# Low parts of stage-two weights and of the token matrix, summed on TensorE; six weight slots; transfers held back

## The chip, the cores and the metric

The kernel runs on one core of one Trainium2 chip. The time is that of one execution on the device, in microseconds. A core has a matrix engine (TensorE, PE in the profile), three engines for elementwise work (VectorE or DVE, ScalarE or ACT, GpSimd or POOL), and SyncE (SP), whose queue issues every transfer of this kernel.

## The reference

Three stages run over 8 batches of 576 tokens: an attention with softmax on each side, a feed-forward layer with a gate over tokens, and one with a convolution over tokens.

```python
# stage one: 8 heads of 64
q_s = softmax(q, over d);  k_s = softmax(k, over tokens)
x = q_s @ (k_s^T @ v)                        # per batch and head, then 576 x 512
# stage two
h = gelu(x @ w_in)                           # 512 -> 1024
u, v = h[..., :512], h[..., 512:]
v_n = (v - mean) / sqrt(var + 1e-6) * g_ln
v_s = w_sg @ v_n + b_sg                      # 576 x 576 over the tokens
x = x + (u * v_s) @ w_out
# stage three
h = relu(x @ w_in2)                          # 512 -> 1024
out = (h * sigmoid(conv3(h))) @ w_out2       # three taps over the tokens
```

## The kernel before

Each product of two float32 matrices is made of three matmuls in the one-piece type F32R. A matrix is held as a high part (its value rounded to F32R) and a low part (what the rounding left), and `mm3` adds high x high, high x low and low x high. So every operand has to be split before it is used. For activations this is a copy on ScalarE for the high part and a subtraction for the low one. The weights `w_in`, `w_out`, `w_in2`, `w_out2` arrive as 64-bit numbers: `split` (a "job") loads 512 columns of 64-bit words, takes them apart with integer operations on VectorE and ScalarE into a leading value `a` and a remainder `lf`, rounds `a` to `hi` on ScalarE, and makes the low part in two elementwise steps, `a - hi` and then `+ lf`, each on VectorE or GpSimd as the string `MODES_` says.

Stage two has 12 such jobs: 0 to 3 are the `v` half of `w_in`, 4 to 7 its `u` half, 8 to 11 `w_out`. A job needs a slot of SBUF for its raw words and its `a`; there are three, in buffers that later hold the tokens of batch 1 (`xh`, `xl`) and one operand of batch 1 (`lt`), so job 3 waits for job 0's slot. The token matrix `w_sg` is loaded in four blocks of 128 rows and one of 64 into `x2s`, and split by `sg_split` and `sg_tail` into `sgh`, `sgl` and `rhs`; `b_sg` goes into two rows of `rhs`.

Work of stages one and two in a batch is a list of 29 groups: `hv` (tokens times the `v` half, 12 matmuls of 512 columns each, four tiles and a pair tile for the left-over 64 tokens), `hu` (the `u` half, eight units of 12 matmuls of 288 columns), `mx` (the token matrix, 14 matmuls), `wo` (times `w_out`, 12 matmuls). `insert` puts stage one of later batches between them: `attend_k` and `attend_q` (the softmax steps on VectorE, GpSimd and ScalarE), `back_kv` (k times v on TensorE), `xt` and `xt_left` (q times that, which makes the tokens of the next batch). Stage three follows for all batches.

Nothing runs in the order of the code. `Plan` records every instruction, gives each a cost, and works out for each how late it may start (`late`) from where its consumer stands among TensorE's units. `Plan.order` then plays the program forward: a free engine takes the waiting instruction with the earliest `late`; TensorE takes the first unit of the next eight that would hardly stall. Each engine then has that fixed order on the chip. SP is such an engine too, with one line to memory of 200 KB per us. All instructions are issued from one line (L394 in the rows below), so they are told apart by the names of their tiles.

Two names in the rows need a word: `xLh` is also the tile of the identity matrix at the start, and `sgh` and `sgl` first hold q and k of batch 0.

Of the kernel before, what the change touches and what calls it, by code (L numbers as in the profile page):

```python
# [30 lines left out]
class View:  # L31
# [46 lines left out]
    def region(self):  # L78
        n = self.tile.n
        ids = self.ids  # L80
        col = ids.reshape(ids.shape[0], -1)[0] % n if ids.size < 4000 else np.unique(ids[0]) % n
# [60 lines left out]
class Plan:  # L142
    WINDOW = 8

    def __init__(self, real):
# [55 lines left out]
    def price(self, n, out, ins):  # L201
# [9 lines left out]
        elif e == "pe":  # L211
            m = size(out)
            if name == "transpose":
                n.cost = 0.22
            elif ins[0].tile.dtype == F32:
                n.cost = 0.09 if m == 65 else 0.71 if m == 512 else 0.19
            else:
                n.cost = max(0.111, 0.0045 + m * 0.000447)
            n.lat = n.cost + 0.17
        elif e == "act":  # L220
            n.cost = 0.13 + cols * 0.00086
            n.lat = n.cost + 0.12
            f = args_func(n)
            n.table = {"Gelu_apprx_tanh": "g", "Exp": "e", "Sigmoid": "s"}.get(f)
        elif e == "pool":
            if "tensor" in name:
                n.cost = 0.55 if cols == 1 else 0.2 + cols * (0.0008 if name == "tensor_copy" else 0.00195)
# [27 lines left out]
    def order(self):  # L255
# [41 lines left out]
        def start(n, t):  # L297
# [3 lines left out]
            if n.eng == "dve" and n.shared and poolend[0] > t:  # L301
                more = min(cost, poolend[0] - t) * 0.8
                cost, lat = cost + more, lat + more
# [5 lines left out]
            if n.eng == "dve" and n.shared:  # L309
                vecend[0] = t + cost  # L310
            if n.eng == "sp":
                s = max(t + 0.4, wire[0])
                wire[0] = s + n.kb / 200
                lat = wire[0] + 1.9 - t
            n.t, n.done = t, t + lat
            free[n.eng] = t + cost
# [24 lines left out]
        while events:  # L341
# [4 lines left out]
            while again:  # L346
                again = False
                for k in self.real:
                    if free[k] > t + 1e-9:
                        continue  # L350
                    if k == "pe":
# [22 lines left out]
                        continue  # L374
                    can = [n for n in queue[k] if n.ready <= t + 1e-9]
                    if can:
                        key = lambda n: (n.late + (2.0 if n.table and n.table != table[0] else 0.0), n.i)
# [25 lines left out]
def attn_gated_conv_kernel(ctx, tc, q, k, v, q0, k0, w_in, g_ln, w_sgT, b_sg, w_out, w_in2, conv_w, w_out2, out):  # L403
# [47 lines left out]
    def split(slot, src, hi, lo, n, modes, stores=(), behind=None):  # L451
# [24 lines left out]
        if hi is None:  # L476
            dve.tensor_tensor(lo, a, lf, ALU.add)
            return
        modes[0].tensor_tensor(a, a, r32(hi), ALU.subtract)
        modes[1].tensor_tensor(lo, a, lf, ALU.add)  # L480
# [38 lines left out]
    lt2 = [p1.tile([128, DM], F32R, name=f"lt2{i}") for i in range(2)]  # L519
    vn_hi = p1.tile([128, 4, DM], F32R, name="vnh")  # L520
    vn_lo = p1.tile([128, 4, DM], F32R, name="vnl")
    kvd = p1.tile([128, 4, 128], F32, name="kvd")
# [309 lines left out]
    xL = {}  # L832
    ident = p1.tile([128, 256 * 2], F32, tag="xLh")[:, 0:128]
    make_identity(nc, ident.real())
# [91 lines left out]

    bview = b_sg.rearrange("(o t) -> o t", o=1)
# [10 lines left out]
    def sg_bias():  # L938
        for e in range(2):
            o = 64 - 64 * e  # L940
            sp.dma_start(sgs[o:o + 2, 1], bview.to_broadcast([2, S]))

# [27 lines left out]
    xt_copy(0)  # L970
    for i, jb in enumerate(jobs):
        split(slots[i % 3], *jb, MODES[i])
        if i == 7:
            split(csl[0], conv_v, None, cw, 3 * NFC, None)
    s_sg()

    def sg_split(c):
        act.activation(sg["hi"][:, c], sgs[:, c % 2], AF.Copy)
        E[CFG['sgl'][c]].tensor_tensor(sg["lo"][:, c], sgs[:, c % 2], r32(sg["hi"][:, c]), ALU.subtract)
        if c < 3:  # L980
            sg_load(c + 2)
        if c == 3:
            sg_bias()

    def sg_tail():
        act.activation(rhs1, sgs[:, 0], AF.Copy)
        bsh = sgs[:, 0].bitcast(F32R)
        for e in range(2):
            r = slice(64 * e, 64 * e + 64)
            E[CFG['rh'][e]].tensor_tensor(rhs2[e][r], sgs[r, 0], r32(rhs1[r]), ALU.subtract)  # L990
        for e in range(2):
            o = 64 - 64 * e
            act.activation(bsh[o:o + 2], sgs[o:o + 2, 1], AF.Copy)
            dve.tensor_tensor(rhs2[e][o:o + 2], sgs[o:o + 2, 1], r32(bsh[o:o + 2]), ALU.subtract)
            dve.tensor_copy(rhs2[e][o:o + 1], r32(bsh[o:o + 1]))

    w2 = {}

    NW = 256
    wsl = p1.tile([128, 1792], F32, name="wsl")  # L1000
    parts = [((wsl[:, 512 * i:512 * i + 512], wsl[:, 1024 + NW * i:1024 + NW * i + NW]), wsl[:, 1536:1792]) for i in range(2)]
# [106 lines left out]
    for b in range(B):  # L1108
# [196 lines left out]
```

## Time and profile before

| what | value |
|---|---|
| median of 3 runs | 1012.88 us (1011.97 to 1016.14) |
| profiled execution, its own time | 1012.38 us |
| its span in the profile | 1010.6 us |
| mean granted clock of TensorE | 0.966 |
| TensorE busy | 932.2 us, 92% of the span |
| VectorE busy | 758.2 us, 75% |
| ScalarE, GpSimd busy | 471.7 us, 386.6 us |

The span is what the trace covers; the execution's own time is 1.8 us longer. Busy shares are means over stages: stages one and two of all batches run to about 600 us, stage three from there. A clock of 1.00 is 2.4 GHz, and 0.50 is 1.2 GHz. A wait in the rows is the time that an engine stood before an instruction, with the instruction that ended it.

### The profile page before, as it was taken

What the parts mean: (1) busy time and instruction counts of PE and PEld (TensorE: products, weight loads), DVE (VectorE), ACT (ScalarE), POOL (GpSimd) and SP (SyncE); (2) the same over time, 40 slices, a digit from 0 to 9 for tenths busy, and PEclk for the clock granted to TensorE, in tenths of its full rate; (3) what the DMA queues carried; (4) which work ended last, traced back from release to release, by engine and by line L of the source; (5) the groups of instructions that cost most, each with busy time, mean ns of one, the idle gap of its engine ahead of it and who ended that gap; (6) DMA issues with size and microseconds to landing.
All of it is one profiled execution on the core that took longest, in us unless ns stands there. A gap on an engine that the chain in (4) does not pass through costs nothing. (4 is left out here: it accounts for less than half of the span.)

```text
span 1010.6 us, 16155 instructions
## 1 busy us (share of the span) xinstructions
PE 932.2 (92%) x6080; PEld 836.1 (83%) x6080; DVE 758.2 (75%) x1361; ACT 471.7 (47%) x913; POOL 386.6 (38%) x469
## 2 busy tenths in 40 slices
PE   5456689999998998999999999999999999999998
PEld 3246578898887987989889999898999899989996
DVE  7999989878898895895763539977677757775663
ACT  5546434766755637545451315434343434343432
POOL 5666465645465552643540104442222312210000
PEclk9676989999999998999999999999999999999999
DMA  9702514251462442614327452332211211010001
GB/s 285 226 28 84 167 72 144 94 153 52 127 192 81 165 116 73 215 53 159 103 96 240 149 163 114 119 111 74 73 68 68 89 58 69 22 42 11 22 22 52
DMA packets 52326, 107.41 MB, mean 106 GB/s; under 512 B 5140, under 2 KB 28692, under 8 KB 48664
## 3 DMA queue, kind: packets, MB, share of 16 engines
q1 hardware_dynamic: 52248, 106.38, 32.6%
q8 instruction: 47, 0.77, 0.3%
q14 instruction: 31, 0.25, 0.1%
HBM read 70.85 MB, written 35.52 MB: 105 GB/s over the span
## 5 line engine op out<-in xcount | busy, mean ns | idle before, releaser
L394 PE MATMUL mm<-xh,w2h 128*128 128x288 f32 x512 | 151.3, 295 | 0.0
L394 PE MATMUL mm<-xh,w2l 128*128 128x288 f32 x512 | 151.1, 295 | 0.0
L394 PE MATMUL mm<-xl,w2h 128*128 128x288 f32 x512 | 150.6, 294 | 0.0
L394 DVE SCALAR_TENSOR_TENSOR cv<-h,cw,cv 128x576 f32<-128x576 f32 x128 | 117.5, 918 | 4.0
L394 ACT ACTIVATE cv<-cv 128x576 f32<-128x576 f32 x64 | 43.9, 686 | 138.2 <-DVE cv L394 138.2
L394 PE MATMUL acc<-wAh,yl 128*128 128x512 f32 x256 | 101.5, 396 | 0.0
L394 PE MATMUL acc<-wAh,yh 128*128 128x512 f32 x256 | 101.4, 396 | 0.0
L394 PE MATMUL acc<-wAl,yh 128*128 128x512 f32 x256 | 101.0, 394 | 0.0
L394 PEld LDWEIGHTS mm<-xl,w2h 128*128 128x128 f32 x512 | 96.6, 189 | 2.5
L394 PEld LDWEIGHTS mm<-xh,w2h 128*128 128x128 f32 x512 | 96.1, 188 | 2.5
L394 PEld LDWEIGHTS mm<-xh,w2l 128*128 128x128 f32 x512 | 96.3, 188 | 0.0
L394 PE MATMUL mm<-xh,wAh 128*128 128x288 f32 x256 | 80.7, 315 | 15.6 <-ACT wAh L394 11.3
L394 PE MATMUL mm<-sgh,vnh 128*128 128x288 f32 x256 | 81.8, 319 | 8.6 <-DVE xl L394 8.6
L394 DVE TENSOR_TENSOR yl<-cv,yh 128x576 fp32r<-128x576 f32 x64 | 51.9, 810 | 47.9 <-ACT yh L394 44.7
L394 PE MATMUL mm<-xh,wAl 128*128 128x288 f32 x256 | 77.6, 303 | 4.9 <-POOL wAl L394 4.8
L394 PE MATMUL acc<-gh,wouth 128*128 128x288 f32 x256 | 80.9, 316 | 0.3 <-ACT gh L394 0.3
L394 DVE TENSOR_TENSOR cv<-cv,h 128x576 f32<-128x576 f32 x64 | 51.8, 809 | 38.0 <-ACT cv L394 37.9
L394 PE MATMUL acc<-gh,woutl 128*128 128x288 f32 x256 | 76.6, 299 | 3.6 <-DVE woutl L394 3.6
L394 PE MATMUL acc<-gl,wouth 128*128 128x288 f32 x256 | 77.3, 302 | 2.8 <-DVE gl L394 2.7
L394 PE MATMUL mm<-xl,wAh 128*128 128x288 f32 x256 | 77.4, 302 | 0.0
L394 PE MATMUL mm<-sgh,vnl 128*128 128x288 f32 x256 | 77.1, 301 | 0.3 <-DVE vnl L394 0.3
L394 POOL TENSOR_TENSOR q<-q,qm 128x512 f32<-128x512 f32 x56 | 63.0, 1151 | 37.1 <-DVE qm L394 30.9
(188 smaller groups left out, 2533.0 us busy)
## 6 DMA issues: line engine op xcount, KB each, us to landing
vt<-in_v SPq DMA_DIRECT2D x8, 1152.0 KB, 11.5
x2d<-x2s SPq DMA_DIRECT2D x16, 576.0 KB, 4.0
out<-ot SPq DMA_DIRECT2D x32, 256.0 KB, 2.1
kt<-in_k SPq DMA_DIRECT2D x7, 1152.0 KB, 6.6
xld<-xl SPq DMA_DIRECT2D x7, 1152.0 KB, 4.7
xf<-x2d SPq DMA_DIRECT2D x7, 1152.0 KB, 5.4
xg<-xld SPq DMA_DIRECT2D x7, 1152.0 KB, 5.1
q<-in_q SPq DMA_DIRECT2D x28, 256.0 KB, 2.7
```

The source lines that it names most:

```text
L394: getattr(self.real[n.eng], n.name)(*[val(a) for a in n.args], **{k: val(v) for k, v in n.kw.items()})
```

## The change

The low part of each of the 12 jobs is summed in PSUM by three matmuls, identity x `a`, minus identity x `hi` and identity x `lf`, and copied out by ScalarE. The first and the last are in full F32 (two pieces in the trace), the middle one in F32R. The token matrix is treated alike, with two matmuls for each of ten halves of 288 columns. `b_sg` is split in a small tile and goes to `rhs` by way of device memory. The jobs have six slots: a tile `wsl` and, for jobs 0 and 1, the two tiles that later hold the normalised `v` (`vnh`, `vnl`). Jobs 4 to 11 and the blocks of the token matrix are placed among the groups of batch 0. Stage one of batch 1 is placed later in batch 0, and `attend`, `back_kv` and `xt_left` of later batches at groups 24 to 27 in place of 19 to 25. In the planner some costs change (ScalarE's, GpSimd's smallest operation, VectorE's loss beside GpSimd), and a transfer is held back while the line to memory is taken for more than 1 us ahead, unless its `late` is within 30 us.

```diff
@@ class Plan
+    AHEAD = 30.0
...
             if n.eng == "sp":
+                heapq.heappush(events, max(t, wire[0] - 1.0) + 0.01)
                 s = max(t + 0.4, wire[0])
                 wire[0] = s + n.kb / 200
                 lat = wire[0] + 1.9 - t
+                heapq.heappush(events, wire[0] - 0.99)
...
                     can = [n for n in queue[k] if n.ready <= t + 1e-9]
+                    if k == "sp" and wire[0] > t + 1.0:
+                        now = t if first >= len(units) else units[first][0].late
+                        can = [n for n in can if n.late < now + self.AHEAD]
...
@@ split
+        if modes is None:
+            plan.begin()
+            ps = mm_tile()
...
+            pe.matmul(ps, one, a, start=True, stop=False)
+            pe.matmul(ps, neg, hi, start=False, stop=False)
+            pe.matmul(ps, one, lf, start=False, stop=True)
+            act.activation(lo, ps, AF.Copy)
+            return
         modes[0].tensor_tensor(a, a, r32(hi), ALU.subtract)
         modes[1].tensor_tensor(lo, a, lf, ALU.add)
...
+    one = p1.tile([128, 128], F32, name="one")
+    ident = one
...
+    neg = p1.tile([128, 128], F32R, name="neg")
+    act.activation(neg, one, AF.Copy, scale=-1.0)
...
-    slots = [(sa[:, 0:1024], sb[:, 1024:1536]), (sa[:, 1024:2048], sb[:, 1536:2048]), (sb[:, 0:1024], st3)]
+    wsl = p1.tile([128, 1792], F32, name="wsl")
+    early = [p1.tile([128, 4 * DM], F32, tag=f"vn{n}") for n in "hl"]
+    slots = [(sa[:, 0:1024], sb[:, 1024:1536]), (sa[:, 1024:2048], sb[:, 1536:2048]), (sb[:, 0:1024], st3), (wsl[:, 0:1024], wsl[:, 1024:1536])]
+    slots += [(t[:, 0:1024], t[:, 1024:1536]) for t in early]
...
-    for i, jb in enumerate(jobs):
-        split(slots[i % 3], *jb, MODES[i])
-        if i == 7:
-            split(csl[0], conv_v, None, cw, 3 * NFC, None)
+    def w_job(i):
+        split(slots[ORDER[i]], *jobs[i], None)
+
+    ORDER = (4, 5, 0, 1, 2, 3, 0, 1, 2, 3, 0, 1)
+    for i in range(4):
+        w_job(i)
+    vn_hi = p1.tile([128, 4, DM], F32R, tag="vnh")
+    vn_lo = p1.tile([128, 4, DM], F32R, tag="vnl")
+    split(csl[0], conv_v, None, cw, 3 * NFC, None)
...
     def sg_split(c):
         act.activation(sg["hi"][:, c], sgs[:, c % 2], AF.Copy)
-        E[CFG['sgl'][c]].tensor_tensor(sg["lo"][:, c], sgs[:, c % 2], r32(sg["hi"][:, c]), ALU.subtract)
+        for hf in range(2):
...
+            part(ps, sgs[:, c % 2, cs], sg["hi"][:, c, cs])
+            act.activation(sg["lo"][:, c, cs], ps, AF.Copy)
...
+    def part(ps, x, hi):
+        pe.matmul(ps, one, x, start=True, stop=False)
+        pe.matmul(ps, neg, hi, start=False, stop=True)
...
@@ insert, and the loop over batches
-            if b == 0 and i in (8, 9):
-                back_kv(1, i - 8)
-            if b == 0 and i == 10:
+            if b == 0 and i in (14, 15):
+                back_kv(1, i - 14)
+            if b == 0 and i == 16:
                 xt_left(1)
-            if i in ((12, 14, 16, 18) if b % 2 == 0 else (8, 10, 12, 14)):
-                xt(b + 1, (i - (12 if b % 2 == 0 else 8)) // 2)
+            at_ = 17 if b == 0 else 12 if b % 2 == 0 else 8
+            if i in (at_, at_ + 2, at_ + 4, at_ + 6):
+                xt(b + 1, (i - at_) // 2)
             if b + 2 < B:
-                if i == 19:
+                if i == 24:
                     attend_k(b + 2)
                     attend_q(b + 2)
-                if i in (23, 24):
-                    back_kv(b + 2, i - 23)
-                if i == 25:
+                if i in (25, 26):
+                    back_kv(b + 2, i - 25)
+                if i == 27:
                     xt_left(b + 2)
...
-            if b == 0 and i == 3:
-                for c in range(4):
-                    sg_split(c)
+            if b == 0 and i in (4, 5, 7, 9):
+                w_job(4 + (4, 5, 7, 9).index(i))
+            if b == 0 and i in (3, 4, 5, 6):
+                sg_split(i - 3)
+            if b == 0 and i == 6:
                 sg_tail()
+            if b == 0 and i in (10, 11, 12, 13):
+                w_job(8 + i - 10)
```

On TensorE, these are the rows at the start of stage two, before and then with the change: the first rows are stage one of batch 0 (`q` times `kvd`), and `wAh` x `xh` is the first `hv` tile.

```order
L394 MATMUL mm_151<-q_0_225,kvd_89 128x512
L394 MATMUL mm_175<-q_0_232,kvd_89 128x512
L394 MATMUL mm_187<-q_0_242,kvd_89 128x512
L394 MATMUL mm_133<-q_0_315,kvd_89 128x64 x4
L394 MATMUL mm_151<-wAh_238,xh_0_306 128x512
L394 MATMUL mm_151<-wAl_261,xh_0_306 128x512
L394 MATMUL mm_151<-wAh_238,xl_0_320 128x512
L394 MATMUL mm_151<-wAh_238,xh_0_306 128x512
L394 MATMUL mm_151<-wAl_261,xh_0_306 128x512
```

```order
L403 MATMUL mm_186<-q_0_239,kvd_91 128x512
L403 MATMUL mm_138<-q_0_277,kvd_91 128x64 x4
L403 MATMUL mm_153<-vnh_121,one_80 128x512
L403 MATMUL mm_153<-wAh_299,neg_87 128x512
L403 MATMUL mm_153<-vnh_121,one_80 128x512
L403 MATMUL mm_174<-vnl_124,one_80 128x512
L403 MATMUL mm_174<-wAh_299,neg_87 128x512
L403 MATMUL mm_174<-vnl_124,one_80 128x512
L403 MATMUL mm_186<-xl_0_133,one_80 128x512
L403 MATMUL mm_186<-wAh_299,neg_87 128x512
L403 MATMUL mm_186<-xh_0_127,one_80 128x512
L403 MATMUL mm_138<-xl_0_133,one_80 128x512
```

With the change, four times three matmuls (slots `vnh`, `vnl` and the two in `xl`/`xh`) stand between stage one and the first `hv` tile; the other eight triples and the ten pairs for the token matrix stand among later rows, before batch 1's `hv`.

On VectorE, the rows around the first job, before and then with the change; `sm` belongs to the softmax of q, and `mm` with `rs` to the division after `back_kv`.

```order
L394 RECIPROCAL sm_115<-sm_115 128x8
L394 TENSOR_SCALAR xl_0_122<-xh_0_112 128x512
L394 TENSOR_REDUCE sm_115<-sgh_91 128x8
L394 TENSOR_SCALAR sm_115<-sm_115 128x8
L394 RECIPROCAL sm_115<-sm_115 128x8
L394 TENSOR_TENSOR sgh_91<-sgh_91,sm_115 128x512
L394 SCALAR_TENSOR_TENSOR xl_0_122<-xh_0_112,xl_0_122 128x512 x2
L394 TENSOR_SCALAR xh_0_112<-xl_0_122 128x512
L394 TENSOR_TENSOR xl_0_122<-xl_0_122,wAh_238 128x512
```

```order
L403 TENSOR_SCALAR sm_117<-sm_117 128x4
L403 RECIPROCAL sm_117<-sm_117 128x4
L403 TENSOR_SCALAR vnh_121<-vnh_121 128x512
L403 SCALAR_TENSOR_TENSOR vnh_121<-vnh_121 128x512
L403 TENSOR_SCALAR rs_0_264<-mm_174 128x2
L403 RECIPROCAL rs_0_264<-rs_0_264 128x2
L403 TENSOR_TENSOR kvd_91<-mm_174,rs_0_264 64x2x64 x2
L403 SCALAR_TENSOR_TENSOR vnh_121<-vnh_121 128x512
L403 TENSOR_SCALAR vnh_121<-vnh_121 128x512
L403 TENSOR_SCALAR vnl_124<-vnl_124 128x512
```

The subtraction `xl<-xl,wAh` (and the sum that made `wAl`, on GpSimd for this job) is gone, and the first job stands behind the softmax of q instead of in it; two jobs are worked on at once.

On SP, the rows from the eighth transfer on, before and then with the change; `vt` is v of a batch, `sgh` the left-over part of q, `kt` k of batch 1, `q_1` q of batch 1.

```order
L394 DMA xh_0_112<-in_w_in 128x1024
L394 DMA vt_85<-in_v 128x36x64
L394 DMA sgh_91<-in_q 128x256
L394 DMA xh_0_112<-in_w_in 128x1024
L394 DMA xl_0_122<-in_w_in 128x1024
L394 DMA x2s_124<-in_w_sgT 128x576 x2
L394 DMA g_bc_128<-in_g_ln 128x512
L394 DMA q_1_135<-in_q 128x256
L394 DMA q_1_140<-in_q 128x512
L394 DMA q_1_143<-in_q 128x512
L394 DMA q_1_147<-in_q 128x512
```

```order
L403 DMA vt_85<-in_v 128x36x64
L403 DMA sgh_93<-in_q 128x256
L403 DMA vnh_121<-in_w_in 128x1024
L403 DMA vnl_124<-in_w_in 128x1024
L403 DMA xh_0_127<-in_w_in 128x1024 x2
L403 DMA x2s_131<-in_w_sgT 128x576
L403 DMA xl_0_133<-in_w_in 128x4x256
L403 DMA g_bc_140<-in_g_ln 128x512
L403 DMA wsl_146<-in_w_in 128x4x256
L403 DMA x2s_131<-in_w_sgT 128x576
L403 DMA bt_319<-in_b_sg 64x9
L403 DMA kt_150<-in_k 128x2304
```

The four loads of jobs 0 to 3 stand together ahead of the token matrix and of `q_1`; `q_1` has moved behind the loads of jobs 4 to 8, and `vt` ahead of the first job.

## Rows read from the trace of the kernel before

**Rows 1.** the page: busy time, share of the span and instructions of each engine

```profile
PE 932.2 (92%) x6080; PEld 836.1 (83%) x6080; DVE 758.2 (75%) x1361; ACT 471.7 (47%) x913; POOL 386.6 (38%) x469
```

**Rows 2.** stretches: length, PE, PEld, DVE, ACT, POOL busy (count), PEclk, DMA share, GB/s

```profile
32.00:96.90 64.90, 32.39 (x154) 25.67 (x154) 62.67 (x91) 36.30 (x67) 45.10 (x35) 0.68 0.30 91
96.90:160.00 63.10, 50.23 (x399) 45.29 (x400) 58.50 (x133) 25.98 (x52) 33.49 (x32) 0.89 0.44 136
160.00:600.00 440.00, 424.34 (x2998) 385.93 (x2997) 328.87 (x725) 230.08 (x456) 195.71 (x220) 0.99 0.41 129
600.00:1010.60 410.60, 405.97 (x2405) 366.49 (x2404) 284.59 (x367) 160.81 (x305) 96.05 (x156) 1.00 0.19 66
```

**Rows 3.** who ended TensorE's waits from 32 to 160 us: total, times, longest

```profile
PE mm L394 <- ACT wAh L394: 17.9, 2, 11.3
PE mm L394 <- DVE xl L394: 8.6, 1, 8.6
PE mm L394 <- DVE wAl L394: 6.9, 2, 4.2
PE mm L394 <- POOL wAl L394: 4.8, 1, 4.8
PE acc L394 <- DVE woutl L394: 3.6, 1, 3.6
```

**Rows 4.** timeline of TensorE, start and duration: first hv matmuls of batches 0, 1

```profile
31.94 0.48 PE L394 MATMUL mm<-wAh,xh 128*128 128x512 f32 x1
...
159.86 0.40 PE L394 MATMUL mm<-wAh,xh 128*128 128x512 f32 x1
160.09 0.39 PE L394 MATMUL mm<-wAl,xh 128*128 128x512 f32 x1
```

**Rows 5.** VectorE by form, 0 to 150 us: busy, mean ns, idle before

```profile
L394 DVE TENSOR_TENSOR wAl<-xl,xh 128x512 fp32r<-128x512 f32 x3 | 3.9, 1300 | 0.1
...
L394 DVE TENSOR_TENSOR xl<-xl,wAh 128x512 f32<-128x512 f32 x3 | 3.6, 1188 | 0.5 <-ACT wAh L394 0.5
...
L394 DVE TENSOR_TENSOR lt<-lt,wAh 128x512 f32<-128x512 f32 x2 | 2.5, 1242 | 0.1
L394 DVE TENSOR_TENSOR rhs<-x2s 2x576 fp32r<-2x576 f32 x2 | 2.3, 1158 | 0.0
```

**Rows 6.** GpSimd instructions by form, 0 to 150 us

```profile
L394 POOL TENSOR_TENSOR sgl<-x2s,sgh 128x576 fp32r<-128x576 f32 x3 | 5.5, 1845 | 0.0
...
L394 POOL TENSOR_TENSOR xl<-xl,wAh 128x512 f32<-128x512 f32 x3 | 4.7, 1577 | 0.8 <-ACT wAh L394 0.8
...
L394 POOL TENSOR_TENSOR wAl<-xl,xh 128x512 fp32r<-128x512 f32 x3 | 3.9, 1306 | 0.8 <-DVE xl L394 0.7
L394 POOL TENSOR_TENSOR wAl<-lt,xl 128x512 fp32r<-128x512 f32 x2 | 3.6, 1794 | 0.1
```

**Rows 7.** TensorE timeline: 512-column matmuls in one piece, an F32 one in two

```profile
38.34 0.63 PE L394 MATMUL mm<-wAh,xh 128*128 128x512 f32 x1
38.77 0.63 PE L394 MATMUL mm<-wAl,xh 128*128 128x512 f32 x1
...
178.62 1.02 PE L394 MATMUL mm<-q,kvd 128*128 128x512 f32 x2
```

**Rows 8.** timeline of TensorE: one key-value product and one left-over product

```profile
149.53 1.83 PE L394 MATMUL mm<-vt,kt 128*64 128x65 f32 x40
...
152.99 1.00 PE L394 MATMUL mm<-q,kvd 128*128 128x64 f32 x8
```

**Rows 9.** ScalarE by form, 0 to 150 us: copies out of PSUM into F32R

```profile
L394 ACT ACTIVATE xh<-mm 128x512 fp32r<-128x512 f32 x8 | 4.6, 596 | 5.5 <-PE mm L394 3.7 <-DVE woutl L394 1.8
```

**Rows 10.** timeline of VectorE: the same operation twice

```profile
25.00 0.40 DVE L394 TENSOR_SCALAR xl<-xh 128x512 uint32<-128x512 uint32 x1
...
87.16 2.87 DVE L394 TENSOR_SCALAR xl<-xh 128x512 uint32<-128x512 uint32 x1
```

**Rows 11.** DMA issues: loads of w_in, KB each, us to landing

```profile
xh<-in_w_in SPq DMA_DIRECT2D x6, 512.0 KB, 5.8
```

More of the change, by code (lines that the diff above doesn't have):

```diff
@@ L80, in region @@
         ids = self.ids
+        if self.tile.space == "dram":
+            ids = np.unique(ids)
+            ids = np.stack(np.broadcast_arrays(np.unique(ids // n)[:, None] * n, np.unique(ids % n)[None])).sum(0)
         col = ids.reshape(ids.shape[0], -1)[0] % n if ids.size < 4000 else np.unique(ids[0]) % n
@@ L220, in price @@
         elif e == "act":
-            n.cost = 0.13 + cols * 0.00086
+            n.cost = 0.15 + cols * 0.00091
             n.lat = n.cost + 0.12
@@ L226, in price @@
             if "tensor" in name:
-                n.cost = 0.55 if cols == 1 else 0.2 + cols * (0.0008 if name == "tensor_copy" else 0.00195)
+                n.cost = 0.8 if cols == 1 else 0.2 + cols * (0.0008 if name == "tensor_copy" else 0.00195)
             else:
@@ L301, in start @@
             if n.eng == "dve" and n.shared and poolend[0] > t:
-                more = min(cost, poolend[0] - t) * 0.8
+                more = min(cost, poolend[0] - t) * 1.0
                 cost, lat = cost + more, lat + more
@@ L478, in split @@
             return
+        if modes is None:
+            plan.begin()
+            ps = mm_tile()
+            if len(src.shape) == 4:
+                ps = ps.rearrange("p (g f) -> p g f", g=g)
+            pe.matmul(ps, one, a, start=True, stop=False)
[3 more added lines that the diff above has]
+            return
         modes[0].tensor_tensor(a, a, r32(hi), ALU.subtract)
@@ L519, in attn_gated_conv_kernel @@
     lt2 = [p1.tile([128, DM], F32R, name=f"lt2{i}") for i in range(2)]
-    vn_hi = p1.tile([128, 4, DM], F32R, name="vnh")
-    vn_lo = p1.tile([128, 4, DM], F32R, name="vnl")
     kvd = p1.tile([128, 4, 128], F32, name="kvd")
@@ L832, in attn_gated_conv_kernel @@
     xL = {}
-    ident = p1.tile([128, 256 * 2], F32, tag="xLh")[:, 0:128]
-    make_identity(nc, ident.real())
+    one = p1.tile([128, 128], F32, name="one")
+    ident = one
+    make_identity(nc, one.real())
+    neg = p1.tile([128, 128], F32R, name="neg")
+    act.activation(neg, one, AF.Copy, scale=-1.0)
     sa = xp.tile([128, 2304], F32, tag="xh1")
@@ L925, in s_xl @@
             pool.memset(r32(xL[n][:, :, 64:128]), 0.0)
-    bview = b_sg.rearrange("(o t) -> o t", o=1)
     sgs = wk.tile([128, 2, S], F32, tag="x2s", bufs=1)
@@ L936, in sg_load @@
                 sp.dma_start(sgs[r, 0], w_sgT[512:576])
[L938 to L941, printed above, removed]
     def s_sg():
@@ L978, in sg_split @@
         act.activation(sg["hi"][:, c], sgs[:, c % 2], AF.Copy)
-        E[CFG['sgl'][c]].tensor_tensor(sg["lo"][:, c], sgs[:, c % 2], r32(sg["hi"][:, c]), ALU.subtract)
+        for hf in range(2):
+            cs = slice(hf * HALF, hf * HALF + HALF)
+            plan.begin()
+            ps = mm_tile()[:, 0:HALF]
+            part(ps, sgs[:, c % 2, cs], sg["hi"][:, c, cs])
+            act.activation(sg["lo"][:, c, cs], ps, AF.Copy)
         if c < 3:
             sg_load(c + 2)
-        if c == 3:
-            sg_bias()
     def sg_tail():
         act.activation(rhs1, sgs[:, 0], AF.Copy)
[L987 to L990, printed above, removed]
+        for hf in range(2):
+            cs = slice(hf * HALF, hf * HALF + HALF)
+            plan.begin()
+            ps = mm_tile()[:, 0:HALF]
+            part(ps, sgs[:, 0, cs], rhs1[:, cs])
+            for e in range(2):
+                r = slice(64 * e, 64 * e + 64)
+                act.activation(rhs2[e][r, cs], ps[r], AF.Copy)
+        bt = p1.tile([128, 9], F32, name="bt")[0:64]
+        bh = p1.tile([128, 9], F32R, name="bh")[0:64]
+        bl = p1.tile([128, 9], F32R, name="bl")[0:64]
+        bd = dram.tile([128, S], F32, name="bd")
+        sp.dma_start(bt, b_sg.rearrange("(p f) -> p f", f=9))
+        act.activation(bh, bt, AF.Copy)
+        dve.tensor_tensor(bl, bt, r32(bh), ALU.subtract)
+        for i, t in enumerate((bh, bl)):
+            sp.dma_start(bd[i:i + 1].rearrange("o (p f) -> (o p) f", f=9), r32(t))
         for e in range(2):
             o = 64 - 64 * e
-            act.activation(bsh[o:o + 2], sgs[o:o + 2, 1], AF.Copy)
-            dve.tensor_tensor(rhs2[e][o:o + 2], sgs[o:o + 2, 1], r32(bsh[o:o + 2]), ALU.subtract)
-            dve.tensor_copy(rhs2[e][o:o + 1], r32(bsh[o:o + 1]))
+            sp.dma_start(r32(rhs2[e][o:o + 2]), bd[0:2])
+    def part(ps, x, hi):
+        pe.matmul(ps, one, x, start=True, stop=False)
+        pe.matmul(ps, neg, hi, start=False, stop=True)
     w2 = {}
     NW = 256
-    wsl = p1.tile([128, 1792], F32, name="wsl")
     parts = [((wsl[:, 512 * i:512 * i + 512], wsl[:, 1024 + NW * i:1024 + NW * i + NW]), wsl[:, 1536:1792]) for i in range(2)]
```

## Prediction

> **What bounds the kernel now.** The page's first line says TensorE is busy 92% of the span and VectorE 75% [rows 1], so the question is where the other 8% of TensorE lies. The stretches answer it: from 160 to 600 us TensorE is busy 424.3 of 440 us at a clock of 0.99, and from 600 us 406.0 of 410.6 at 1.00, but from 32 to 160 us it is busy 82.6 of 128 at clocks of 0.68 and 0.89 [rows 2]. In that stretch VectorE is busy 62.7 + 58.5 = 121.2 of 128 us: there it is the bound, and TensorE waits 45.4 us for it. The list of who ended TensorE's waits there names the results of the weight jobs: high and low parts of w_in (wAh 17.9, wAl 6.9 and 4.8), the low part of w_out (3.6), and once the next batch's tokens (xl 8.6) [rows 3]. ScalarE and GpSimd stand in the list as the last link of chains that VectorE feeds. So I time the stretch from batch 0's first hv matmul at 31.9 us to batch 1's at 159.9 us [rows 4], and take what follows as it is.
>
> How much of it does TensorE need? Busy time times clock gives an estimate at full rate: 32.4 x 0.68 + 50.2 x 0.89 = 66.7 us. Of the 82.6 busy us the other 15.9 are lost to the lower clock.
>
> **What VectorE loses.** Of the 24 elementwise steps of the 12 jobs' low parts, 13 are on VectorE and 11 on GpSimd. Rows show eight of the 13: 3.9 + 3.6 + 2.5 us, and the two-row pieces of b_sg another 2.3 [rows 5]; that is 12.3. Nine smaller pieces have no row here (five subtractions and sums, one block of the token matrix, one half of its tail, two one-row copies). They lie between 0.40 us, the quickest 512-column operation shown [rows 10], and the listed mean of 12.3 / 10 = 1.2, so between 3.6 and 11; I take 6, near the low end because two are one row and some ran alone. VectorE loses 18 us (16 to 23).
>
> GpSimd loses its 11 job steps, three blocks of the token matrix and the other half of the tail: 5.5 + 4.7 + 3.9 + 3.6 = 17.7 us in rows [rows 6] and four single ones. This helps VectorE too: the same TENSOR_SCALAR took 0.40 us once and 2.87 us another time [rows 10]. How much of VectorE's time such meetings take has no row of its own. The bounds are nothing and us for us, 17.7. I take 5, about a quarter, since GpSimd was busy 45.1 + 33.5 = 78.6 us in the stretch [rows 2] and still VectorE did all its other work. GpSimd keeps one multiplication per job.
>
> **What TensorE gains in work.** An F32R matmul of 512 columns follows the one before after 0.23 us at the full clock [rows 4] and 0.43 at half [rows 7]. An F32 one is two pieces and took 1.02 us [rows 7], of which 0.40 - 0.23 = 0.17 is the tail that the next overlaps, so 0.85; at half I double it to 1.7. A job is then 0.85 + 0.23 + 0.85 = 1.9 us (3.8 at half), and twelve are 23. A half of the token matrix is (0.85 + 0.23) x 288/512 = 0.6, and ten are 6. Together 29 us at full clock, 58 at half. Four jobs, 7.7 us, stand ahead of the first hv, which therefore begins later than now: 31.9 + 7.7 = 39.6 us. (Their loads take 5.8 us to land [rows 11] and now stand ahead of the token matrix and q_1; VectorE's share of four jobs is done by about that time too, since it has no low parts to make, so I put no extra wait there.) Eight jobs, 15.4, and the 6 for the token matrix come inside the stretch. Work moved out of it: the key-value products of batch 2 (two of 1.83 us) and its left-over product (1.00) [rows 8] now stand behind batch 1's first hv, 4.7 us.
>
> **What ScalarE gains.** Twelve copies out of PSUM at 0.60 us [rows 9] and twelve of 288 columns at no more than that: at most 14.4 us. ScalarE is busy 36.3 + 26.0 = 62.3 of 128 us [rows 2], so this is covered by its idle time; if a copy came last in a chain, each such place would cost its 0.6.
>
> **What is moved or held.** Stage one of batch 1 goes to later groups. This is where the 8.6 us wait for xl stood [rows 3]; the new order puts mx, wo and hu units between the four xt, so I count that wait as part of the 45.4 that the two sums below replace. Holding transfers back costs nothing while the line has room: the DMA engines are 30% and 44% busy in the stretch [rows 2]. If the room is missed, the slots show it: jobs 6 and 7 load only when TensorE has read jobs 2 and 3 at about 40 us, 5.8 us to landing, and behind them in SP's queue stand the b_sg pieces, v of batch 1, two blocks of the token matrix, jobs 8 and 9 and q_1. Ahead of the hu units that need jobs 6 and 7, TensorE has the hv tiles and the pair (60 x 0.23), jobs 4 and 5 (3.8) and eight halves of the token matrix (4.8), 22 us; less the landing, some 16 us are cover for the two chains. The b_sg round trip (a load, two stores, a load back) has those 22 us and more until the first mx. The new planner costs change no duration, only the order.
>
> **The sum.** TensorE alone: 39.6 + 66.7 + 15.4 + 6 - 4.7 = 123.0 us for batch 1's first hv at full clock without a wait; with half of the present loss to the lower clock (8 us, since there are fewer waits) 131. VectorE alone: 31.9 + 128 - 18 - 5 = 136.9. The later one decides: 137 us against 159.9 now. Of the 22.9, 4.7 is only moved, so the gain is 18.2 us. From 160 us on I keep the 15.7 us that TensorE lacks up to 600 [rows 2]; with another order in every batch it may be 6 us more or less. The profiled execution took 1012.4 us, 0.5 below the median; 1012.4 - 18.2 = 994. By the bounds: VectorE down by 23 + 17.7 leaves 119, so TensorE's 123 to 125 decides, and the time is 982; the two engines within a few us of each other, so that each waits for the other 10 us more, gives 1004. The likeliest case's own range is 987 to 1002.
>
> **A rule weighed.** The operation that took 0.40 us alone took 2.87 beside GpSimd [rows 10]: that is a stall, not a slower rate. The Trainium skill, SBUF — State Buffer, section Who interferes with whom, says that VectorE and GpSimd share a pair of ports as a lock: a VectorE operation with two inputs in SBUF, or in a two-port mode, waits until GpSimd's whole instruction is done, and the other way round. The row agrees in kind. By that rule in full, each us taken from GpSimd could come off VectorE, 17.7 where I count 5, and the sum would be 982.
>
> **The rivals.**
> 1. GpSimd's steps blocked VectorE us for us. VectorE's sum falls to 31.9 + 128 - 18 - 17.7 = 124, TensorE's 123 to 125 decides, 982. For it: the 2.87 us. Against: VectorE did 121 us of work beside 78.6 of GpSimd's. 0.14.
> 2. Late loads or latency in the chains. A slot serves two or three jobs, each a chain of some eleven instructions on four engines with a load ahead of it; TensorE and VectorE are both near their bounds, so a late link is no longer covered. 10 us of waits in place of the 45 removed: 147 us, 1004. For it: TensorE's waits now hang on such chains [rows 3]. 0.15.
> 3. Slower: TensorE at half clock becomes the bound. If all of the added work runs at half (58 us) and the present loss of 15.9 stays, hv of batch 1 comes at 31.9 + 15.3 + 66.7 + 15.9 + 30.6 + 12 - 4.7 = 168 us, 13 us late with the 4.7: 1025. It decides from 155 us on, that is when lower clock and waits cost over 32 us beyond the 123. For it: the clock is 0.68 to 97 us [rows 2]. Against: it is low where TensorE waits, and the new matmuls fill these waits. 0.06.
> 4. It does nothing: the waits move to the token matrix and the next batch, and the gain is under 5 us. 0.07. Against: the bound is VectorE's work, and 18 us of it are gone.
>
> **Numbers.** The forecast holds 0.58 (987 to 1002). Differences under 0.5%, 5 us, can't be told from none here. Faster by more: 0.58 + 0.14 + 0.14 of the second = 0.86; the same 0.08; slower 0.06. The range 981 to 1006 holds the forecast, the first rival and the second; about 0.2 is left out with the last two and the ends.
>
> **What would show it.** Batch 0's first hv near 40 us; the 11.3 us wait for wAh gone; batch 1's first hv at 130 to 145; the clock from 32 to 97 us above 0.8; F32 matmuls of the identity at 0.85 to 0.9 us; VectorE's busy time before 160 us down by some 20. Wrong would be: waits for xl, gl or a load of over 10 us before 140; identity matmuls at 1.7; or more than 22 us of TensorE idle from there to 600.

## The result, and the profile after

The changed kernel took 979.38 us (median of 4 runs, 975.98 to 985.53) beside 1013.85 for the kernel before in the same session: 0.9666 of the time, interval 0.9612 to 0.972. That is 34 us less where 18 were forecast, and just below the range of 981 to 1006. The ratios in this document leave out one execution, of the last version told of below, which took 3225.91 us where its others took 971.83 to 974.22; why, no trace shows.

The profiled execution is the slowest of the four, 985.53 us. Its line of busy times, to be read beside [rows 1]:

```profile
PE 953.3 (97%) x6170; PEld 847.7 (86%) x6170; DVE 737.3 (75%) x1343; ACT 487.4 (50%) x941; POOL 358.6 (36%) x454
```

VectorE lost 21 us and TensorE gained 21. The stretches, cut at batch 0's first `hv`, batch 1's first `hv` and the start of stage three; columns as in [rows 2], the first row being the stretch that [rows 2] begins with:

```profile
32.00:96.90 64.90, 61.60 (x270) 42.85 (x269) 56.42 (x101) 51.84 (x97) 30.00 (x28) 1.00 0.40 118
...
0.00:41.95 41.95, 29.99 (x153) 18.30 (x153) 28.25 (x57) 25.95 (x49) 17.39 (x30) 1.00 0.67 212
41.95:140.66 98.71, 91.28 (x533) 73.77 (x531) 84.60 (x174) 63.09 (x117) 45.89 (x45) 0.95 0.46 136
140.66:573.48 432.82, 426.37 (x3091) 389.47 (x3089) 341.34 (x749) 237.01 (x472) 199.31 (x224) 0.99 0.43 135
573.48:983.80 410.32, 405.70 (x2402) 366.14 (x2400) 283.12 (x366) 161.31 (x305) 95.99 (x156) 1.00 0.19 66
```

The same cuts in the kernel before, which [rows 2] cuts at round numbers:

```profile
31.94:159.86 127.92, 82.54 (x551) 70.88 (x551) 121.08 (x224) 62.34 (x118) 78.45 (x66) 0.79 0.37 113
159.86:600.50 440.64, 424.98 (x3002) 386.57 (x3001) 329.50 (x726) 230.08 (x456) 195.85 (x220) 0.99 0.41 128
600.50:1010.60 410.10, 405.47 (x2402) 365.99 (x2400) 284.09 (x366) 160.81 (x305) 96.05 (x156) 1.00 0.19 66
```

Batch 1's first `hv` comes 19.2 us earlier (140.66 for 159.86). The stretch behind it is 7.8 us shorter (432.8 for 440.6), though work that the prediction prices at 4.7 us has moved into it (3091 matmuls for 3002). Stage three is the same. 19.2 + 7.8 - 0.2 = 26.8 us, the difference of the two spans. The chain of the first stretch is cleared: from 32 to 97 us TensorE is busy 61.6 of 64.9 us at a clock of 1.00 instead of 32.4 at 0.68. Who ended its waits, from 32 to 140 us and then (behind the dots) from 140 to 573 us:

```profile
PE acc L403 <- DVE gl L403: 2.7, 1, 2.7
PE mm L403 <- DVE kvd L403: 2.2, 1, 2.2
PE mm L403 <- ACT wAl L403: 1.4, 2, 1.0
PE mm L403 <- ACT sgh L403: 1.1, 1, 1.1
...
PE mm L403 <- DVE u L403: 3.6, 2, 2.9
PE acc L403 <- DVE gl L403: 1.3, 2, 0.7
```

Of the 17.9 us for `wAh` and of the 8.6 for `xl` [rows 3] 0.3 us each is left. TensorE's idle time behind batch 1's `hv` is 432.8 - 426.4 = 6.4 us, where it was 440.6 - 425.0 = 15.7.

### The profile page after: what moved, and what is told of

It is laid out like the page before. It is cut to its first block, busy times and chain, and to the rows that moved or that the text cites. A ratio compares the mean times of both kernels' runs of the same rounds, so it can differ in the third digit from the quotient of the medians.

```text
span 983.8 us, 16326 instructions
## 1 busy us (share of the span) xinstructions
PE 953.3 (97%) x6170; PEld 847.7 (86%) x6170; DVE 737.3 (75%) x1343; ACT 487.4 (50%) x941; POOL 358.6 (36%) x454
## 4 chain that ended last, share of the span: by engine, by line
PE 85%; DVE 9%; ACT 3%; issue 1%; DMA 0%; SPq 0%; POOL 0%; ACTq 0%
PE mm L403 58%; PE acc L403 28%; DVE scr L403 1%; DVE r L403 1%; ACT L403 1%; DVE wsl L403 1%; DVE gl L403 1%; DVE lt L403 1%; DVE lm L403 1%; DVE xl L403 1%; DVE qm L403 0%; DVE lx L403 0%; DMA sgh<-in_q 0%; ACT q L403 0%; DVE sm L403 0%
## 5 line engine op out<-in xcount | busy, mean ns | idle before, releaser
L403 PE MATMUL acc<-gh,wouth 128*128 128x288 f32 x256 | 82.9, 324 | 0.0
L403 PE MATMUL mm<-sgl,vnh 128*128 128x288 f32 x256 | 75.7, 296 | 0.0
## 6 DMA issues: line engine op xcount, KB each, us to landing
vt<-in_v SPq DMA_DIRECT2D x8, 1152.0 KB, 10.2
```

The lines of the kernel that those rows point to most:

```text
L403: getattr(self.real[n.eng], n.name)(*[val(a) for a in n.args], **{k: val(v) for k, v in n.kw.items()})
```

## The experiments

All ratios are to the kernel before; 0.005 is 5 us. "The two points" are batch 1's first `hv` and the start of stage three.

**The changed kernel once more**, beside the next three, for a second profile.

> The changed kernel once more. Its profiled execution took 985.5 us and the other three 976 to 981, so this shows where an execution differs. If the difference is the clock after short waits of TensorE: the stretch before batch 1's first hv is 4 to 8 us shorter at a clock near 1.00, the rest within 1 us. If it is the waits themselves: the waits for kvd and gl of 2.2 and 2.7 us in that stretch are gone.

979.53 us, 0.9662 (0.9633 to 0.9691). Its stretches:

```profile
0.00:38.48 38.48, 26.45 (x153) 16.05 (x153) 28.40 (x57) 26.12 (x49) 17.40 (x30) 1.00 0.75 232
38.48:135.68 97.20, 89.76 (x533) 72.19 (x531) 84.54 (x174) 63.02 (x117) 45.79 (x45) 0.96 0.47 138
135.68:566.11 430.43, 423.88 (x3091) 387.24 (x3089) 341.24 (x749) 237.27 (x472) 200.06 (x224) 1.00 0.44 135
```

This execution is nearer the median and is the one that the others are held against: points at 135.7 and 566.1 us. Against before that is 24.2 us up to the first, 10.2 behind it. Neither expectation came: the same waits for `kvd` and `gl` stand in it, and of the 5.0 us at the first point 3.5 lie ahead of batch 0's first `hv`.

**Low parts back on VectorE and GpSimd**, everything else as changed:

```diff
-        split(slots[ORDER[i]], *jobs[i], None)
+        split(slots[ORDER[i]], *jobs[i], MODES[i])
```

and likewise `sg_split` and `sg_tail` as before.

> The change with its six slots, new places, held-back transfers and new planner costs, but the low parts of the 12 jobs and of the token matrix made on VectorE and GpSimd again. Theory A (two sources: the low parts off VectorE shorten the stretch up to batch 1's first hv by about 20 us, the planner's numbers and places shorten the stretch to 600 us by about 12): 995 to 1005 us, batch 1's first hv near 155 to 160 us. Theory B (all of it comes from the planner's side, since TensorE pays 29 us for the low parts): 976 to 986. Theory C (all of it comes from the low parts, through less contention between VectorE and GpSimd): 1008 to 1014.

993.51 us, 0.9796 (0.9773 to 0.982). So the sums on TensorE are worth 13.6 us of the 34. The first stretch and the waits in it:

```profile
36.90:144.39 107.49, 76.57 (x438) 66.48 (x438) 102.05 (x173) 46.17 (x91) 65.61 (x57) 0.81 0.37 111
```

```profile
PE mm L403 <- DVE u L403: 11.9, 4, 4.8
PE mm L403 <- DVE wAl L403: 6.1, 3, 4.3
PE mm L403 <- POOL wAl L403: 5.5, 2, 4.2
```

VectorE is the bound again, 102 of 107.5 us, and TensorE waits 11.6 us for `wAl`. Batch 1's first `hv` stands at 144.4 us, not at 155 to 160 as expected: slots, places and planner bring 15.5 of the 24.2 us up to it without the sums.

**The planner's part alone**, in the kernel before: the new costs, the hold, and the later places for stage one of batches 2 on. And **the reverse**: the changed kernel without costs, hold and places (for batches 3 on).

```diff
-            n.cost = 0.13 + cols * 0.00086
+            n.cost = 0.15 + cols * 0.00091
...
-                n.cost = 0.55 if cols == 1 else ...
+                n.cost = 0.8 if cols == 1 else ...
...
-                more = min(cost, poolend[0] - t) * 0.8
+                more = min(cost, poolend[0] - t) * 1.0
...
+                        can = [n for n in can if n.late < now + self.AHEAD]
...
-                if i == 19:
+                if i == 24:
...
```

> The kernel before with the planner's new costs, transfers held back, and attend, back_kv and xt_left of batches 2 and up at groups 24 to 27; three slots and low parts on VectorE and GpSimd as before. Theory A: 998 to 1006, the gain lying behind batch 1's first hv. Theory B: 980 to 990. Theory C: 1010 to 1016.

> The change with the planner's old costs, no transfer held back, and attend, back_kv and xt_left of batches 3 and up at their old groups 19 to 25; low parts on TensorE and six slots stay. Theory A: 988 to 995, with the stretch from batch 1's first hv to stage three near 440 us again. Theory B: 1000 or more. Theory C: 976 to 984.

Planner alone: 1001.01 us, 0.9871 (0.9842 to 0.9899), 13 us. Without it: 1004.04 us, 0.9899 (0.9874 to 0.9923), 10 us. Together they give 34, so 11 us come only from both. In the first, the stretch to batch 1's `hv` hardly moves and the one behind it shrinks by 10.4 us:

```profile
31.57:158.55 126.98, 82.70 (x548) 70.94 (x549) 119.23 (x214) 61.50 (x109) 73.27 (x63) 0.78 0.35 107
158.55:588.82 430.27, 421.28 (x3003) 384.14 (x3002) 342.38 (x735) 234.07 (x467) 199.25 (x222) 1.00 0.43 134
```

In the second that stretch is 447.5 us long, and one wait of 13.7 us for the token matrix's high part stands at the start:

```profile
PE mm L403 <- ACT sgh L403: 14.9, 2, 13.7
```

**The planner's three parts, each taken out of the changed kernel**: old costs; no hold (`AHEAD = 1e12`); old places for stage one of batches 3 on.

> The change with the planner's old costs alone. Costs theory (the new costs make the order fit the chip, which takes about 10 us out of the stretch from batch 1's first hv to stage three): 986 to 991 us, that stretch at 437 us or more instead of 430. Places theory (the later groups for attend, back_kv and xt_left do that): 977 to 982, the stretch at 430 to 432.

> The change without held-back transfers. Hold theory (the wait of 13.7 us for the first block of the token matrix in the run with the old planner comes from transfers that are not urgent standing ahead of it): 988 to 995, with a wait of 8 to 14 us for sgh before batch 1's first hv. Rival (that wait came from the old costs, which made the loads look less urgent): 977 to 982, no such wait.

> The change with attend, back_kv and xt_left of batches 3 and up at their old groups 19 to 25. Places theory: 985 to 991, the stretch from batch 1's first hv to stage three at 437 or more. Costs theory: 977 to 983.

Old costs: 996.37 us, 0.9821 (0.9801 to 0.9841), 16 us lost. No hold: 991.16, 0.9774 (0.9758 to 0.979), 11 lost. Old places: 979.69, 0.9662 (0.9631 to 0.9693), nothing. With the old costs the first point is where it was, and the loss lies behind it, 450.7 us for 430.4. TensorE idles 16.0 of these (6.6 before the edit), and is busy 10.9 us longer, at a clock of 0.98 for 1.00 and with 10 matmuls more:

```profile
38.45:133.66 95.21, 86.64 (x521) 69.40 (x520) 78.56 (x165) 62.20 (x116) 43.62 (x42) 0.99 0.47 141
133.66:584.36 450.70, 434.74 (x3101) 394.66 (x3101) 344.62 (x757) 242.62 (x476) 201.78 (x226) 0.98 0.42 129
```

Without the hold TensorE waits 10.7 us for `sgh` in the first stretch. The timeline of ScalarE without the hold:

```profile
66.54 1.28 ACT L403 ACT_TABLE_LOAD   x1
68.47 2.12 ACT L403 ACTIVATE kt<-kt 128x2304 f32<-128x2304 f32 x1 [0.65 <-POOL kt L403]
70.50 0.67 ACT L403 ACTIVATE sgh<-x2s 128x576 fp32r<-128x576 f32 x1
```

With the hold that copy ran at 58.87 us. Its load was issued at 49.3 us without the hold and at 48.6 with it, so no late load explains it: what differs is that ScalarE does `kt` of batch 1 first (with the hold, `kt` comes at 83.5 us). The ten `q_1` loads were issued from 21 to 40 us without the hold, and from 55 us on with it; what the hold changes is when they come, and with it the order on the other engines; which of them put `kt` first was not tried apart.

**Low parts on TensorE alone**, in the kernel before: three slots, all jobs ahead of the groups, old planner.

```diff
...
-        split(slots[i % 3], *jb, MODES[i])
+        split(slots[i % 3], *jb, None)
...
```

> The kernel before with the low parts of the jobs and of the token matrix on TensorE and nothing else: three slots, all jobs ahead of batch 0's groups in the code, old planner. If VectorE's relief is what counts at the start: 1003 to 1008, batch 1's first hv at 150 to 155. If it needs the jobs spread over the groups of batch 0 (TensorE's triples stand in its fixed order, and nine of them ahead of the first hv make it wait for VectorE): 1010 to 1025, batch 0's first hv at 60 us or later.

1028.53 us, 1.0138 (1.0117 to 1.016): slower. The job sums now stand in TensorE's order ahead of the first `hv`, which comes at 91 us; up to there TensorE is busy 26 of 60 us and waits for the jobs' values:

```profile
PE mm L394 <- DVE xl L394: 30.1, 3, 26.3
```

**Which engine bounds the start now?** Three edits of the changed kernel: the remainder `lf` written as F32R, so that the third sum is one piece; the token matrix's low parts alone made elementwise again; both.

```diff
-        (pool if hi is not None else dve).tensor_tensor(lf, lf, hf, ALU.mult)
+        rem = lo if modes is None and hi is not None else lf
+        (pool if hi is not None else dve).tensor_tensor(rem, lf, hf, ALU.mult)
...
-            pe.matmul(ps, one, lf, start=False, stop=True)
+            pe.matmul(ps, oner, lo, start=False, stop=True)
...
+    act.activation(oner, one, AF.Copy)
```

> The changed kernel, with the remainder of the bf16 rounding written as F32R, so that a job's third sum runs on TensorE in one piece instead of two. Between 32 and 97 us TensorE is busy 61.6 of 64.9 us in the changed kernel. If TensorE is now what bounds the start, twelve jobs of 512 columns give back about 0.4 us each at the full clock, some 5 to 7 us, all ahead of batch 1's first hv: that hv at 129 to 132 us instead of 136 to 141, the whole at 973 to 976 us. If VectorE or ScalarE bounds it, the waits on them grow by the same and the whole stays at 979. A job's remainder rounded to F32R moves nothing else.

> The changed kernel, with the low parts of the token matrix alone (not of the stage-two weights) made element by element on VectorE and GpSimd again. TensorE loses about 6 us of sums, VectorE and GpSimd get the token matrix's operations back. If TensorE alone bounds the start: 973 to 976 us. If VectorE is as close (its sum in the forecast was 137 us, TensorE's 123 to 131): within 3 us of 979. If contention between VectorE and GpSimd counts: 982 to 987.

> Both edits of the two runs beside it: the remainder of a job in F32R and the token matrix's low parts element by element. If TensorE bounds the start up to batch 1's first hv, the two add up: 968 to 972 us. If VectorE takes over after the first 5 us, it stands with the better of the two, 973 to 977 us, and the waits on VectorE between 32 and 140 us grow.

Remainder in F32R: 987.46 us, 0.9726 (0.9703 to 0.975), slower than the changed kernel. Token matrix elementwise: 975.72, 0.9608 (0.9582 to 0.9635), faster. Both: 978.68, 0.9641 (0.9619 to 0.9663), outside both expected ranges; its first point is at 132.7 us, with 7.3 us of waits for `rhs` ahead of it. The first takes 5.4 us off TensorE up to the first point (84.3 busy for 89.8), but that point moves by 0.8 us only, since the waits for `sgh` grow to 7.7. The second:

```profile
38.21:125.61 87.40, 78.10 (x478) 61.52 (x476) 80.53 (x156) 48.43 (x96) 47.59 (x45) 1.00 0.51 148
125.61:563.48 437.87, 430.48 (x3112) 393.31 (x3113) 351.03 (x769) 233.21 (x471) 205.55 (x228) 0.99 0.43 134
```

Here TensorE has 11.7 us less to do in the first stretch and that stretch is 9.8 us shorter. So TensorE bounds it in that order; in the other run its saving came back as waits. Behind it 6.6 us more TensorE work and a longer wait for `u` (7.4 for 3.6 us) take most of it back.

**Which cost, and why?** One cost put back at a time; then all three moved on by one step, and far past the rows; then another price, that of F32 matmuls on TensorE.

```diff
 f1   n.cost = 0.13 + cols * 0.00086                      (ScalarE)
 f2   n.cost = 0.55 if cols == 1 ...                      (GpSimd)
 f3   more = min(cost, poolend[0] - t) * 0.8              (VectorE beside GpSimd)
 f4   0.17 + cols * 0.00096;  1.05;  1.2                   (all one step on)
 f5   0.25 + cols * 0.00116;  2.05;  2.0                   (all far past)
 h1   n.cost = ... 0.86 if m == 512 else 0.48 if m == 288 ... (0.71 and 0.19 in the changed kernel)
```

> The changed kernel with ScalarE's planner cost alone put back (0.13 + 0.00086 a column for 0.15 + 0.00091). All three costs put back took 17 us off the gain. The cost of a 512-column operation differs by 0.05 us, where the trace of before shows 591 to 723 ns against 570 planned before and 616 now. If what counts is that each cost is near what the trace shows, this one, wrong by the least, is worth 0 to 6 us: 979 to 985. If any other set of costs is merely another draw of the order: anywhere from 979 to 996, with no relation to how wrong the cost is.

> The changed kernel with GpSimd's smallest operation alone put back to 0.55 us in the planner (0.8 now; the trace of before shows 966 ns for it, 32 times, in the chain to the normalised v). If the costs' truth counts, most of the 17 us is here: 988 to 996, with TensorE waiting more for what follows the normalisation. If it is a draw of the order: anywhere from 979 to 996.

> The changed kernel with VectorE's loss beside GpSimd alone put back (0.8 for 1.0 of the time that the two share). If truth counts, 2 to 10 us: 981 to 989. If it is a draw of the order: anywhere from 979 to 996.

> The changed kernel with all three costs moved on by as much again (ScalarE 0.17 + 0.00096 a column, GpSimd's smallest 1.05, the loss 1.2). 0.17 + 0.49 = 0.66 us for 512 columns and 1.05 lie as near to the rows (591 to 723 ns, 966 ns) as the new costs do. If truth counts: within 5 us of 979. If it is a draw of the order: 980 to 1000, most likely slower, since the new numbers would be a lucky one.

> The changed kernel with the three planner costs moved far past the rows: ScalarE 0.25 + 0.00116 a column (0.84 us for 512 columns against 591 to 723 ns in the trace of before), GpSimd's smallest 2.05 us (966 ns), VectorE's loss beside GpSimd 2.0 of the shared time. If what counts is nearness to the measured durations: slower than the changed kernel, 984 to 1000. If what counts is only that the planner is told to leave slack: as fast as with the costs moved on by one step, 970 to 978. If it is a draw of the order: anywhere from 972 to 996.

> The changed kernel with the planner's price of one kind of instruction put right: F32 matmuls of 512 columns at 0.86 us (0.71 now) and of 288 columns at 0.48 (0.19 now). The trace of the changed kernel has a job's triple every 1.99 us and a pair of the token matrix every 0.62 us, of which 0.23 and 0.13 are the F32R matmul. The change is the first to use the 288-column ones. If nearness of the prices to the durations counts: 970 to 977, the token matrix's sums being the worst-priced instruction left. If only more slack on VectorE, ScalarE and GpSimd counts: 979 within 3. If orders are a draw: 972 to 996.

| edit | time, us | ratio (interval) | the two points, us |
|---|---|---|---|
| ScalarE's cost back | 987.73 | 0.9748 (0.9729 to 0.9767) | 136.0, 577.6 |
| GpSimd's back | 983.76 | 0.9711 (0.9692 to 0.973) | 128.4, 571.6 |
| VectorE's back | 985.16 | 0.9723 (0.9702 to 0.9743) | 135.1, 574.3 |
| all one step on | 974.74 | 0.9618 (0.9599 to 0.9637) | 129.3, 562.3 |
| all far past | 1005.27 | 0.9901 (0.9887 to 0.9915) | 134.2, 568.0 |
| F32 matmuls priced as measured | 984.29 | 0.9689 (0.9659 to 0.9719) | 132.1, 570.7 |

Each cost put back alone loses 5 to 9 us (8.7, 5.0 and 6.2 by the ratios, 20 in sum, where all three together lose 16), and not by how wrong it was: ScalarE's, the least wrong, counts most. One step further gains another 4.5. Far past, stages one and two end about where they did (568.0 for 566.1), and the 25 us are lost in stage three:

```profile
567.98:1003.10 435.12, 408.39 (x2402) 367.88 (x2400) 295.54 (x394) 171.84 (x326) 112.46 (x177) 0.97 0.22 75
```

```profile
PE acc L403 <- ACT yh L403: 22.2, 1, 22.2
```

Its rows of `wsl`, the raw weights of stage three, run to 601.5 us, where the changed kernel's end at 526.7: this plan put weight preparation off. ScalarE works on it up to 599.5 us and makes `yh`, for which the first product with `w_out2` waits, after that. The right price for TensorE's F32 matmuls, a test of nearness on an engine where a higher price gives the others no slack, did not help (its interval meets the changed kernel's, and lies mostly above it).

**The version that the runs point to**: costs one step on, and the token matrix elementwise.

> The changed kernel with the three costs moved on by one step and the token matrix's low parts made element by element: the two edits that each gained 4 to 5 us. If they add: 969 to 971. If the costs' gain hangs on one order and does not carry to another program: 974 to 980.

973.28 us, 0.9585 (0.9572 to 0.9599), the fastest of all: 8 us below the changed kernel by the ratios. Of the 4.5 and 5.5 us apart, most adds up. Points at 123.9 and 559.4 us.

## Why the prediction was half right

**The bound of before, and the gain up to batch 1's first `hv`: right.** Batch 0's first `hv` at 39.6 forecast, 38.5 and 42.0 measured; batch 1's at 137 forecast (130 to 145), 135.7 and 140.7 measured; the gain up to there 22.9 forecast, 24.2 and 19.2 measured. The wait of 11.3 us for `wAh` is gone, the clock from 32 to 97 us is 1.00, and TensorE's job sums cost what was forecast, 1.9 us a job: the triple of job 4 begins at 54.84 us, and the next unit 1.99 us later.

```profile
54.84 1.02 PE L403 MATMUL mm<-lt,one 128*128 128x512 f32 x2
55.29 0.80 PE L403 MATMUL mm<-wAh,neg 128*128 128x512 f32 x1
55.93 1.06 PE L403 MATMUL mm<-xl,one 128*128 128x512 f32 x2
56.83 0.65 PE L403 MATMUL mm<-x2s,one 128*128 128x288 f32 x2
```

The second to fourth are the rest of the job and the first pair of the token matrix.

**Which engine decides the 137: wrong; that the number held is luck.** VectorE's sum was to decide. It is busy 84.5 of 97.2 us there, TensorE 89.8. VectorE lost 36.5 us in this stretch against the 23 forecast: over the whole span it lost 21 (758.2 to 737.4), and the rest of its work there moved behind batch 1's `hv`, where it has 11.7 us more, and ahead of batch 0's, 4.9 more. Stage one, placed later, takes its elementwise work along, and the sum had no term for that; it counted only the 4.7 us of TensorE's. So VectorE's busy time before 160 us fell by 9.0 us (144.7 to 135.7), not by some 20. TensorE's own sum, 123 to 131, is the nearer one: 38.5 + 89.8 = 128.2 without a wait, and 7.4 of waits.

**Contention: 5 us counted, about 9 on the jobs' own operations.** The 48 512-column integer and remainder steps of the jobs took 43.4 us before and 34.3 after. Two groups by form, of before, after, and of the kernel with the low parts back on VectorE and GpSimd:

```profile
L394 DVE TENSOR_SCALAR xl<-xh 128x512 uint32<-128x512 uint32 x8 | 8.9, 1117 | 0.0
L394 DVE SCALAR_TENSOR_TENSOR xl<-xh,xl 128x512 uint32<-128x512 uint32 x8 | 8.6, 1076 | 0.2
```

```profile
L403 DVE SCALAR_TENSOR_TENSOR xl<-xh,xl 128x512 uint32<-128x512 uint32 x6 | 6.0, 994 | 0.2
...
L403 DVE TENSOR_SCALAR xl<-xh 128x512 uint32<-128x512 uint32 x6 | 4.0, 674 | 0.0
```

```profile
L403 DVE SCALAR_TENSOR_TENSOR xl<-xh,xl 128x512 uint32<-128x512 uint32 x6 | 7.7, 1289 | 0.1
L403 DVE TENSOR_SCALAR xl<-xh 128x512 uint32<-128x512 uint32 x6 | 5.5, 912 | 0.0
```

With GpSimd's steps back the same operations take 912 and 1289 ns for 674 and 994. All 48 take 42.4 us then. So this term is GpSimd's work, about 9 us on these operations where 5 was taken. By the rule of the Trainium skill weighed there (SBUF — State Buffer, section Who interferes with whom), an operation that meets one of the other engine on the shared ports stands until that one is done. Taken in full for every us, as the prediction did, it would have had all 17.7 come off; the trace shows 9.1 on these operations. (The 17.7 also left out the four single steps, 5.8 us in the trace of before.) VectorE's own steps, taken as 18, were 19.7 us in the trace of before, yet over the whole span it lost 20.8 us, not 19.7 + 9.1. The other 8 us came back on other operations: the 64 steps that make `gl` took 37.0 us before and 41.9 after. The first rival, us for us and 982, is not what happened: the time passed 982, but through the stretch behind batch 1's first `hv`.

**The step that failed: "From 160 us on I keep the 15.7 us that TensorE lacks up to 600", and with it "The new planner costs change no duration, only the order".** The sum added 4.7 us there, with 6 either way. The stretch became 10.2 us shorter in the execution nearest the median, 14.9 off the forecast: 9.1 are idle time of TensorE (15.7 to 6.6), the other 5.8 are busy time, with the clock at 1.00 instead of 0.99 (of 440 us, 1% is 4.4). The planner's part alone does most of it in the kernel before: 440.6 to 430.3 us with as many matmuls, 6.7 of it idle time. The costs are the largest part: with the old ones back, and everything else new, TensorE idles 16.0 us there again. Without the hold the stretch is 437.1 us. That the costs change only the order is true; that an order is worth nothing in a stretch where TensorE is 96% busy is what was wrong. The hold was given no gain either: without it the first stretch is 103.2 us long instead of 97.2, and 11 us are lost in all.

**Why the costs help is not settled.** Two of the three were below what the trace of before shows: a ScalarE copy of 512 columns was priced at 0.57 us and took 0.60 [rows 9], and GpSimd's one-column step in the normalisation of `v` at 0.55, now 0.8:

```profile
L394 POOL TENSOR_TENSOR rd<-rd,nhalf 128x1 f32<-128x1 f32 x32 | 30.9, 966 | 71.1 <-DVE rd L394 71.0
```

For VectorE's loss beside GpSimd no row gives the price. One step on, nearer to or past the rows, was better still. But the loss did not go with the error, and the right price of the F32 matmuls did not help. Four of four runs with a cost lowered were slower and the one with all raised a little was faster, as slack on the three engines would have it. Far too much slack cost nothing more than 2 us before stage three, and then 25 by putting other work off.

Against slack as the cause stand edits that touch none of the three costs and lengthen the same stretch. With the remainder in F32R, edited only ahead of batch 1's first `hv`, the stretch behind it has the same 3091 matmuls and is 10.0 us longer:

```profile
134.86:575.32 440.46, 430.23 (x3091) 391.48 (x3089) 345.54 (x749) 239.86 (x475) 199.29 (x225) 0.99 0.43 132
```

The right F32 price gives 438.6 us there, one cost put back 439 to 443 us. And the step further gains ahead of that point (129.3 for 135.7 us), not behind it (433.0 for 430.4). Of the ranges set for nearness, ScalarE's cost back (987.7 for 979 to 985) and GpSimd's back (983.8 for 988 to 996) missed theirs. So these runs do not tell slack from a lucky order of the changed kernel: that the old costs lose 16 us is shown, why is open.

**The other rivals.** Late loads (1004) and TensorE at half clock (1025) did not come: no wait is over 2.7 us from 32 to 140 us, and the clock is 1.00 up to 97 us and 0.95 in the whole stretch up to 140.7. Nor did the waits merely move (the rival of a gain under 5 us). The low parts alone do end on the slower side, 1028 us, by a mechanism that was not among them: sums in TensorE's fixed order ahead of the first `hv`, in a kernel without the slots and the later places.

## What to carry to other kernels

Where a planner fixes the order, price every change of its costs by a run of that change alone, and read the idle time of the bound engine in every stretch: 10 us spread over seven batches weighed nearly as much here as the longest wait (11.3 us). Before a gain is put down to a cost, see what an edit that should not matter does to the same stretch. Compare a planner's costs with the rows' means before calling them harmless. Moving work from a full engine to an idle one pays only where it may stand late enough in the receiver's order; and when the bound has changed, a saving on the new bound must again be tried, since the order it brings can take it back.

## What the runs showed that was not expected

- Two profiled executions of the changed kernel, with nearly the same list of waits, differ by 7.4 us in span (983.8 and 976.4). In part it is the granted clock: the stretch between the `hv` of batches 2 and 3 took 68.46 us at 0.95 in one and 66.18 at 1.00 in the other. In part it is not in that column: up to 41.95 and 38.48 us both show 1.00, yet TensorE was busy 30.0 and 26.5 us with the same 153 matmuls, and the eight `q` x `kvd` pieces took 835 ns each in one and 605 in the other. What slowed them the runs don't show. A gain of 5 us is not to be read from one profile.
- TensorE's granted clock from 32 to 97 us was 0.68 before, with 32.4 us busy, and 1.00 with the change, with 61.6. From 41.95 to 140.66 us it was 0.95, with 91.3 of 98.7 us busy.
- The two halves of the change gave 10 and 13 us apart and 34 together.
